# Relu-squared attention followed by a top-1 expert layer: TensorE's order given to the scheduler, score tiles made five ahead, some high parts on ScalarE, PSUM banks regrouped and the routing steps spread

## The chip, the cores and the metric

The kernel runs on one core of one Trainium2 chip. A core has a matrix engine (TensorE, PE in the profile), a vector engine (VectorE, DVE), a scalar engine (ScalarE, ACT), a general engine (GpSimd, POOL) and SyncE (SP), which in this kernel issues nearly all transfers. Matmuls write to PSUM, which has eight banks of 128 x 512 f32. The metric is the device time of one execution in microseconds. Where profiles are quoted, they come from one profiled execution, whose span runs from its first to its last instruction.

## The reference

B = 8 sequences of S = 2496 positions, 256 values wide, with 64-wide score vectors. Attention without a softmax feeds a layer of E = 8 experts with hidden width 1024, of which each position uses one:

```python
scores = (1.0 / S) * np.matmul(z, z.transpose(0, 2, 1))
attn = np.maximum(scores, 0.0) ** 2
x = (u * np.matmul(attn, v)).reshape(B * S, D)

xn = x / (np.linalg.norm(x, axis=-1, keepdims=True) + 1e-06)
logits = xn @ en.T / tau                 # en: normalised expert_emb
expert_idx = np.argmax(logits, axis=1)   # gate_w: its softmax probability
for e in range(E):
    mask = expert_idx == e
    h = np.maximum(x[mask] @ w1[e], 0.0)
    out[mask] = gate_w[mask, None] * (h @ w2[e])
```

## The kernel before

**Precision.** Matmuls run on f16 operands. Each f32 factor is kept as a sum of a high and a low f16 part, and a product is formed from three matmuls (high x high, high x low, low x high).

**Attention.** A sequence has NG = 5 groups of columns (four of 512, one of 448) and NST = 20 tiles of 128 rows. The main loop goes through `steps`, the 800 triples (b, g, s). In a step, `values` (L328) adds the product of value tile s with the probabilities of (s, g) to two accumulators, k = 0 and 1, of 512 columns: six matmuls (L339 to L341, or L336 and L337 for the last tile). The score matrix of a sequence is symmetric, so only tiles with s // 4 >= g are computed ("own" or direct steps: 20, 16, 12, 8 and 4 of a sequence's groups, 480 in all). The others are taken from `turned` tiles `tt`, which DMA transposes (L317) filled in an earlier group.

An own tile is made in two functions. `scores` (L294) issues two matmuls into a bank `sc` (L299, L300) and has ScalarE take the Relu into `a` (L302) and square it in place (L303). `parts` (L306) has VectorE cast the square to the high part (L309), subtract to get the low part (L310), and, where it is needed later, issues the transpose. At the start of a step the loop calls `scores` for the tile LOOK = 3 own tiles ahead; at its end it calls `parts` for the one LOOK - 1 ahead.

**PSUM.** Pool `psS` has four banks for `sc` and, in the expert stage, `po`; `psA` has three for the accumulators and, in the expert stage, `ph`; `psM` has one, `pm`, for small matmuls.

**Routing.** When a group is done, `route` (L351) returns some two dozen pieces with due times counted in steps: `gate_x` (times u, which reads both accumulators, L369), `squares` (L373), `total` (a `pm` matmul, L378), `scale`, `high` (L393), `low` (L396), `turn` (four transposes into `row`, L401), `logits` (`pm`, L407), `take`, `top`, `rank` (`pm`, L491), `place`, `sums`, four `norm` pieces, the square root, `exps`, `gates` and at 40 steps `scatters` (L516), indirect stores by GpSimd of the rows to an array `xs`, sorted by expert. The pieces wait in `queue`; the loop takes those that are due. Group g's pieces thus run beside the attention of the next groups.

**Beside it.** `ahead` spreads over a sequence the scans of the next sequence's z and v for their largest value, the scales from them (`pm` matmuls L130 and L146), and the loads and splits of z (`z_load` L189, `z_split` L202). Splits of v (`v_split`, L280 and L283) run in the last groups. The weights of the experts are read, split and stored back (`weights`, L526) in small pieces through the first seven sequences. `u_load` (L345) fetches the u of the next group.

**Experts.** Eleven steps before the end of attention `slot_first` (L950) loads the rows and weights of the first slots; a slot holds 256 or 128 rows of one expert. `slot_up` (L899) and `slot_down` (L924) then run slot by slot. Each calls `pop`, which runs one piece that is left in `queue`.

**Order.** The program is traced in the order of these loops. L1000 asks the scheduler to leave TensorE, ScalarE, VectorE and SyncE in just that order; GpSimd isn't in the list. An engine that isn't in it gets its order before the run from the scheduler, which takes of the instructions it holds to be ready the one that stands first in the program. Each engine's order is fixed when the kernel runs.

Of the kernel before, what the change touches and what calls it, by code (L numbers as in the profile page):

```python
# [7 lines left out]
F32 = mybir.dt.float32  # L8
F32R = mybir.dt.float32r
F16 = mybir.dt.float16  # L10
BF16 = mybir.dt.bfloat16
I32 = mybir.dt.int32
U32 = mybir.dt.uint32
AF = mybir.ActivationFunctionType
# [5 lines left out]
P = 128  # L20
TA, TB = 256, 128
ROW = 260
VAHEAD = 6
LOOK = 3
ZMAX, VMAX = 10, 7
SHIFT = 21
NSKIP = 4
# [18 lines left out]
def relu2_attention_then_moe(ctx, tc, zT, uT, v, emb, tau, w1, w2, ident, tri, iota_e, out):  # L46
# [13 lines left out]
    WR1, WR2 = 2 * W1, 2 * W2 + 8  # L60
    KA, KB = slot_counts(B, S, E)
    KT = KA + KB
    assert XFIRST <= NWB - 1 and NWB + 1 <= XAHEAD <= KA
    S2 = float(S) * float(S)
    twin = S % P == DQ
# [4 lines left out]
    dram = ctx.enter_context(tc.tile_pool(name="dram", bufs=1, space=DRAM))  # L70
    cst = ctx.enter_context(tc.tile_pool(name="cst", bufs=1))
    sml = ctx.enter_context(tc.tile_pool(name="sml", bufs=2))
    psS = ctx.enter_context(tc.tile_pool(name="psS", bufs=4, space=PSUM))
    psA = ctx.enter_context(tc.tile_pool(name="psA", bufs=3, space=PSUM))
    psM = ctx.enter_context(tc.tile_pool(name="psM", bufs=1, space=PSUM))

    xs = dram.tile([E * CAP + TB, ROW], F32, name="xs")
# [7 lines left out]
    zpool = actx.enter_context(tc.tile_pool(name="zpool", bufs=2))  # L85
    vring = actx.enter_context(tc.tile_pool(name="vring", bufs=NST + 5))
    wk = actx.enter_context(tc.tile_pool(name="wk", bufs=3))
    tp = actx.enter_context(tc.tile_pool(name="tp", bufs=min(7, max(1, NG * (NG - 1) // 2))))

    Zs = {}  # L90
    Vs = {}
# [202 lines left out]
    def scores(b, g, s):  # L294
        t0, n = groups[g]
        z1, z2 = Zs[b]
        sc = psS.tile([P, 512], F32, name="sc", tag="s")
        ss = slice(s * P, (s + 1) * P)
        nc.tensor.matmul(sc[:, :n], z1[:, ss], z1[:, t0:t0 + n], start=True, stop=False)  # L299
        nc.tensor.matmul(sc[:, :n], z1[:, ss], z2[:, t0:t0 + n], start=False, stop=True)  # L300
        a = wk.tile([P, 512], F32, name="a", tag="a")
        state["at"] = nc.scalar.activation(a[:, :n], sc[:, :n], AF.Relu, scale=2.0 ** -SHIFT).ins  # L302
        nc.scalar.activation(a[:, :n], a[:, :n], AF.Square)  # L303
        return a

    def parts(b, g, s, a):  # L306
        n = groups[g][1]
        hl = wk.tile([P, 2, 512], F16, name="hl_", tag="hl", bufs=5)
        state["dv"] = nc.vector.tensor_copy(hl[:, 0, :n], a[:, :n]).ins  # L309
        nc.vector.tensor_tensor(hl[:, 1, :n], a[:, :n], hl[:, 0, :n], op=ALU.subtract)  # L310
        h = s // GT
        if h > g:
            if (b, g, h) not in turned:
                turned[b, g, h] = tp.tile([P, 2 * GT, 512], F16, name="tt", tag="tt")
            m = min(P, S - s * P)
            c = (s % GT) * P
            nc.sync.dma_start_transpose(turned[b, g, h][:, :, c:c + m], hl[:m].rearrange("p a t -> p (a t)"))  # L317
        return hl[:, 0, :], hl[:, 1, :]
# [32 lines left out]
    def route(b, g, acc, ut):  # L351
# [7 lines left out]
            nc.gpsimd.memset(xhl[:, :, n:nj * P], 0.0)  # L359
        lg = rt.tile([P, 4, E], F32, name="lg", tag="lg")  # L360
        n2 = rt.tile([P, 4], F32, name="n2", tag="n2")
        row = rt.tile([P, 4, ROW + 4], F32, name="row", tag="row")
        rowi = row.bitcast(I32)
        row16 = row.bitcast(F16)
        loc = {}
# [81 lines left out]
            loc["ob"] = ob  # L447

        def sums():
            x = rt.tile([P, 4, D], F32, name="x", tag="x", bufs=1)  # L450
            nc.vector.tensor_tensor(x[:, :nj, :], row16[:, :nj, 0:D], row16[:, :nj, D:2 * D], op=ALU.add)
            loc["x"] = x

        def norm(j):
            def f():
                sq = rt.tile([P, D], BF16, name="sq", tag="sq", bufs=1)
                nc.scalar.activation(sq, loc["x"][:, j, :], AF.Square, accum_out=n2[:, j:j + 1])
            return f
# [37 lines left out]
        def place():  # L496
            ob, pm = loc["ob"], loc.pop("pm")
            state["pm"] = False
            old = state["carry"]
            pos = rt.tile([P, 4, E], F32, name="pos", tag="pos")  # L500
            nc.vector.tensor_tensor(pos[:, :nj, :], pm[:, 0:nj * E].rearrange("p (j e) -> p j e", e=E),
                                    old.unsqueeze(1).broadcast_to([P, nj, E]), op=ALU.add)
            new = sml.tile([P, E], F32, name="carry", bufs=3)
            nc.vector.tensor_tensor(new, pm[:, 4 * E:5 * E], old, op=ALU.add)
            state["carry"] = new
            nc.vector.tensor_tensor(pos[:, :nj, :], pos[:, :nj, :], ob[:, 4:4 + nj, :], op=ALU.mult)  # L506
            dst = rt.tile([P, 4], F32, name="dst", tag="dst")
            nc.vector.tensor_reduce(dst[:, :nj], pos[:, :nj, :], axis=AX.X, op=ALU.add)
            dsti = rt.tile([P, 4], U32, name="dsti", tag="dsti")
            nc.vector.tensor_copy(dsti[:, :nj], dst[:, :nj])  # L510
            loc["dsti"] = dsti

        def scatters():
            for j in range(nj):
# [2 lines left out]
                    xs[:, :], bass.IndirectOffsetOnAxis(ap=loc["dsti"][:m, j:j + 1], axis=0),  # L517
                    row[:m, j, 0:ROW], None)

        return [(0, gate_x), (2, squares), (5, total, True), (6, scale), (8, high), (9, low), (11, turn), (12, logits, True),  # L520
                (13, take), (14, top), (15, rest_scale), (17, rank, True), (18, place), (26, sums)] \
            + [(28 + j, norm(j)) for j in range(nj)] \
            + [(33, root), (34, roots), (35, shifted), (37, exps), (39, gates), (40, scatters)]


    def weights(e):  # L526
# [111 lines left out]
        first_max(c0)  # L638
    probs = {}
    halves = {}  # L640
    for i in range(min(LOOK, len(direct))):
        probs[direct[i]] = scores(*direct[i])
    for i in range(min(LOOK - 1, len(direct))):
        halves[direct[i]] = parts(*direct[i], probs.pop(direct[i]))
    zk = 2
    for k in range(3, min(5, ZN)):
        z_load(0, k * ZC)
    if ZN > 2:
        z_split(0, 2 * ZC)()
        zk = 3  # L650
    for f in scale_pieces(0, "v"):
        at_once(f)


    enhl = cst.tile([P, 2, 2 * E], F16, name="enhl")
    trib = cst.tile([P, P], BF16, name="trib")
    tri_f = sml.tile([P, P], F32, name="tri_f", bufs=1)
    nc.sync.dma_start(tri_f, tri)
    nc.vector.tensor_copy(trib, tri_f)
    ones_b = cst.tile([P, P], BF16, name="ones_b")  # L660
# [200 lines left out]
    mst = {}  # L861
    queue = []

    def pop():
        if queue:
            queue.pop(0)[1]()

    def slot_of(k):
        return (tables["A"], k, TA) if k < KA else (tables["B"], k - KA, TB)
# [108 lines left out]
    def ahead(b):  # L978

        todo = []  # L980
        at = min(4, NB // 16)
        for i, what in enumerate(SCANS):
            todo.append((at + 4 * i, False, lambda w=what: scan_load(b + 1, *w)))
            todo.append((at + 4 * i + 8, False, lambda w=what: scan_max(b + 1, *w)))
        at += 4 * len(SCANS) + 8
        for what, when in (("z", (0, 2, 6)), ("v", (6, 8, 14))):
            for j, (f, w) in enumerate(zip(scale_pieces(b + 1, what), when)):
                todo.append((at + w, j > 0, f))
        at += 10
        gap = max(1, (NB - early - at) // ZN)  # L990
        todo.append((0, False, lambda: z_tiles(b + 1)))
        for k in range(ZN):
            todo.append((max(0, at + (k - 3) * gap), False, lambda k=k: z_load(b + 1, k * ZC)))
            todo.append((at + k * gap, False, lambda k=k: z_split(b + 1, k * ZC)))
        return sorted(todo, key=lambda x: x[0])

    todo = []
    nd = 0
    ET = mybir.EngineType
    ctx.enter_context(tc.manual_schedule(engines={ET.PE, ET.Activation, ET.DVE, ET.SP}))  # L1000
    follow = []
    ready = min(3, NST)
    for s in range(ready):
# [6 lines left out]
    for i, (b, g, s) in enumerate(steps):  # L1010
# [12 lines left out]
            probs[st] = scores(*st)  # L1023
        if s == 0:
            accs[b, g] = [psA.tile([P, 512], F32, name=f"acc{k}", tag="a") for k in range(2)]
            nx = (b, g + 1) if g + 1 < NG else (b + 1, 0)
            if nx[0] < B:
                uts[nx] = u_load(*nx)
            if g == 0 and b + 1 < B:
                todo = ahead(b)  # L1030
        if b == 0 and g == 0 and s + ready < NST:
            follow.append(v_split(b, s + ready))
        if b + 1 < B:
# [16 lines left out]
        else:  # L1050
# [1 line left out]
            if s == 1 and NST > 2:  # L1052
                values(accs[b, g], b, g, 0, *late, ks=(1,))
            values(accs[b, g], b, g, s, *hv, ks=(1,))
        while queue and queue[0][0] <= i:
            pop()
        if wq and i >= wnext and (not wq[0][1] or pm_free(i)):
            wnext += wgap
            follow.append(wq.pop(0)[0]())
# [7 lines left out]
        if s == NST - 1:  # L1067
            queue += [(i + p[0], p[1], len(p) > 2) for p in route(b, g, accs.pop((b, g)), uts.pop((b, g)))]
            if b == B - 2 and g == NG - 1:
                queue.append((i + TABLE, table_a, False))  # L1070
            queue.sort(key=lambda x: x[0])
            pop()
        if own:
            if nd + LOOK - 1 < len(direct):
                st = direct[nd + LOOK - 1]
                halves[st] = parts(*st, probs.pop(st))
            nd += 1
    queue += [(len(steps) + TABLE, table_b, False), (len(steps) + TABLE, pads, False)]
    actx.close()
    slot_pools()  # L1080
    slot_w(1, 1)
# [7 lines left out]
    def work(k0, k1, load=True):  # L1089

        for k in range(k0, k1):
            if k + XAHEAD == KA:
                while queue:
                    pop()
            if k + XAHEAD < k1:
                slot_x(k + XAHEAD)
            slot_up(k)
            if k + NWB < k1:
                slot_w(k + NWB, 0)
            if k > k0:  # L1100
                slot_down(k - 1)
                if k - 1 + NWB < k1:
                    slot_w(k - 1 + NWB, 1)
        slot_down(k1 - 1)
# [79 lines left out]
```

## Time and profile before

| What | us |
|---|---|
| median of 3 runs (2266.07 to 2273.1) | 2268.45 |
| profiled execution | 2270.72 |
| its span, first to last instruction | 2268.8 |
| first value matmul of attention, from the span's start | 22.6 |
| first expert matmul | 1403.06 |
| TensorE, busy as the profile counts it | 2126.3 |
| VectorE busy | 1491.1 |
| ScalarE busy | 1116.7 |

Busy times are those of the whole span. A matmul of 512 columns stands in the profile with about 0.38 us, though the next one starts 0.216 us later; so starts are to be compared, not busy times. In a view of windows each row gives the stretch, its length, then for each engine busy time and number of instructions, the granted TensorE clock, the share of time in which the DMA engines were busy, and what they moved in GB/s. In a list of waits a row gives who waited for whom: total, times, longest. In a timeline a row gives start, duration, engine, line and operation, and in brackets the idle time of the engine before it.

### The profile page before, as it was taken

The numbers are of one execution on the slowest core, as the hardware profiler recorded it, in microseconds if no ns is written. First come the engines' busy times: TensorE is split into PE (matmuls) and PEld (weight loads), VectorE is DVE, ScalarE is ACT, GpSimd is POOL, SyncE is SP. The second block draws the span as 40 slices with busy tenths as digits, with TensorE's granted clock in tenths as the row PEclk, the third lists the DMA queues.
The fourth block names the chain that finished last, engine by engine and source line by source line (L and its number), as shares of the span: only waits on it lengthen the run. The fifth ranks groups of instructions, "written<-read, shape, count | busy, mean of one in ns | idle before, by whom it ended". The sixth has DMA issues, their size and how long they took to land. (4 is left out here: it accounts for less than half of the span.)

```text
span 2268.8 us, 43197 instructions
## 1 busy us (share of the span) xinstructions
PE 2126.3 (94%) x15154; PEld 1349.4 (59%) x15154; DVE 1491.1 (66%) x3972; ACT 1116.7 (49%) x2153; POOL 344.2 (15%) x428
## 2 busy tenths in 40 slices
PE   6998998999988989999999998999999999999997
PEld 2444444444444434444444444888888888889996
DVE  8887888979869879889888775543333333333332
ACT  7676576667747757767767753322222222222221
POOL 0011111011011111111111111132111111112111
PEclk9999999999999999999999999999999999999998
DMA  7967867876874974967885755642233332236561
GB/s 171 195 152 175 174 145 181 170 195 145 186 180 109 208 184 126 228 154 192 175 175 138 133 112 157 163 119 68 48 91 89 88 91 48 56 91 180 123 157 33
DMA packets 610316, 317.85 MB, mean 140 GB/s; under 512 B 530981, under 2 KB 573486, under 8 KB 602928
## 3 DMA queue, kind: packets, MB, share of 16 engines
q1 hardware_dynamic: 594912, 273.82, 53.7%
q0 software_dynamic: 15184, 41.24, 5.5%
q8 instruction: 121, 1.98, 0.4%
q14 instruction: 99, 0.81, 0.1%
HBM read 297.95 MB, written 59.60 MB: 158 GB/s over the span
## 5 line engine op out<-in xcount | busy, mean ns | idle before, releaser
L302 ACT ACTIVATE a<-sc 128x512 f32<-128x512 f32 (+1 forms) x480 | 282.8, 589 | 304.8 <-PE sc L300 175.1
L303 ACT ACTIVATE a<-a 128x512 f32<-128x512 f32 (+1 forms) x480 | 300.8, 627 | 15.1
L340 PEld LDWEIGHTS <-vv 128*128 128x128 f16 x1520 | 149.6, 98 | 233.2 <-issue 80.3
L341 PEld LDWEIGHTS <-vv 128*128 128x128 f16 x1520 | 149.7, 99 | 212.6 <-issue 54.4
L339 PE MATMUL acc<-tt,vv 128*128 128x512 f16 (+1 forms) x640 | 239.7, 375 | 28.9 <-DVE xt L369 22.6
L940 PE MATMUL po<-w,hl 128*128 128x256 f16 x944 | 257.3, 273 | 0.0
L938 PE MATMUL po<-w,hh 128*128 128x256 f16 x944 | 257.3, 273 | 0.0
L939 PE MATMUL po<-w,hh 128*128 128x256 f16 x944 | 257.3, 273 | 0.0
L339 PEld LDWEIGHTS <-vv 128*128 128x128 f16 x1520 | 149.7, 98 | 173.9 <-issue 6.8
L516 POOL DMA_INDIRECT xs<-row,dsti x160 | 172.4, 1078 | 502.1 <-DMA xs<-row,dsti 303.4
L945 POOL DMA_INDIRECT out_dram<-ot,mer x153 | 148.7, 972 | 615.9 <-DVE ot L944 378.2
L341 PE MATMUL acc<-tt,vv 128*128 128x512 f16 (+1 forms) x640 | 239.9, 375 | 0.0
L340 PE MATMUL acc<-tt,vv 128*128 128x512 f16 (+1 forms) x640 | 239.9, 375 | 0.0
L944 DVE TENSOR_SCALAR ot<-po,mer,w 128x256 f32<-128x256 f32 x114 | 58.1, 541 | 197.4 <-PE po L940 197.4
L299 PE MATMUL sc<-z 128*128 128x512 f16 (+1 forms) x480 | 183.1, 381 | 4.3 <-DVE z L215 4.3
L300 PE MATMUL sc<-z,z 128*128 128x512 f16 (+1 forms) x480 | 183.2, 382 | 0.0
L940 PEld LDWEIGHTS <-hl 128*128 128x128 f16 x1272 | 124.5, 98 | 14.4
L938 PEld LDWEIGHTS <-hh 128*128 128x128 f16 x1272 | 124.5, 98 | 14.0
L939 PEld LDWEIGHTS <-hh 128*128 128x128 f16 x1272 | 124.5, 98 | 13.9
L444 POOL MEMSET ob<- 128x72 bf16 x40 | 6.2, 158 | 661.0 <-DVE pos L506 578.5
L939 PE MATMUL po<-wb,hh 128*128 128x256 f16 x328 | 89.4, 273 | 0.0
L940 PE MATMUL po<-wb,hl 128*128 128x256 f16 x328 | 89.4, 273 | 0.0
(4162 smaller groups left out, 5116.9 us busy)
## 6 DMA issues: line engine op xcount, KB each, us to landing
w<-wsd SPq DMA_DIRECT2D x73, 1026.0 KB
wa<-wsd SPq DMA_DIRECT2D x50, 1024.0 KB
w<-wsd SPq DMA_DIRECT2D x48, 1024.0 KB
wb<-wsd SPq DMA_DIRECT2D x25, 1026.0 KB
scan<-in_v_dram SPq DMA_DIRECT2D x56, 312.0 KB
vt<-in_v_dram SPq DMA_DIRECT2D x133, 128.0 KB
ut<-in_uT_dram SPq DMA_DIRECT2D x32, 512.0 KB
wr<-in_w_dram SPq DMA_DIRECT2D x16, 1024.0 KB
```

The lines of the kernel that those rows point to most:

```text
L299: nc.tensor.matmul(sc[:, :n], z1[:, ss], z1[:, t0:t0 + n], start=True, stop=False)
L300: nc.tensor.matmul(sc[:, :n], z1[:, ss], z2[:, t0:t0 + n], start=False, stop=True)
L302: state["at"] = nc.scalar.activation(a[:, :n], sc[:, :n], AF.Relu, scale=2.0 ** -SHIFT).ins
L303: nc.scalar.activation(a[:, :n], a[:, :n], AF.Square)
L339: nc.tensor.matmul(acc[k][:, :n], va, ph[:, :n], start=first, stop=False)
L340: nc.tensor.matmul(acc[k][:, :n], va, pl[:, :n], start=False, stop=False)
L341: nc.tensor.matmul(acc[k][:, :n], vb, ph[:, :n], start=False, stop=last)
L516: nc.gpsimd.indirect_dma_start(xs[:, :], bass.IndirectOffsetOnAxis(ap=loc["dsti"][:m, j:j + 1], axis=0), row[:m, j, 0:ROW], None)
L938: nc.tensor.matmul(o, hh[:, f, t], wh, start=(f == 0), stop=False)
L939: nc.tensor.matmul(o, hh[:, f, t], wl, start=False, stop=False)
L940: nc.tensor.matmul(o, hl[:, f, t], wh, start=False, stop=(f == NF - 1))
L945: nc.gpsimd.indirect_dma_start(out, bass.IndirectOffsetOnAxis(ap=me.bitcast(U32)[:, j, 1:2], axis=0), ot[:, j, :], None, bounds_check=N - ...
```

## The change

- L1000: TensorE leaves the list of engines in program order; ScalarE, VectorE and SyncE stay.
- `LOOK` goes from 3 to 5: scores five own tiles ahead, parts four. The start of the kernel makes five and four tiles accordingly. Buffers: `a` from 3 to 5, `hl_` from 5 to 7, `tt` from 7 to 6.
- `hl_` is now allocated in `scores`; for tiles with s % 3 = 1 ScalarE writes the high part, with a second Square from `a` to f16, and VectorE's cast falls away.
- `psS` has three banks instead of four, `psA` four instead of three.
- The routing pieces lie further apart (`scatters` at 49 instead of 40), `rest_scale` comes before `take`; `row` and `dsti` get a third buffer.
- `u_load` is called at step 3 of a group instead of 0; `z_load` two steps later.
- In the expert stage a call of `pop` counts one step and runs what is due by then, where it ran one piece whatever its due time.
- Two small tiles are renamed or share a buffer.

```diff
-LOOK = 3
+LOOK = 5
...
-    psS = ctx.enter_context(tc.tile_pool(name="psS", bufs=4, space=PSUM))
-    psA = ctx.enter_context(tc.tile_pool(name="psA", bufs=3, space=PSUM))
+    psS = ctx.enter_context(tc.tile_pool(name="psS", bufs=3, space=PSUM))
+    psA = ctx.enter_context(tc.tile_pool(name="psA", bufs=4, space=PSUM))
...
-    tp = actx.enter_context(tc.tile_pool(name="tp", bufs=min(7, max(1, NG * (NG - 1) // 2))))
+    tp = actx.enter_context(tc.tile_pool(name="tp", bufs=min(6, max(1, NG * (NG - 1) // 2))))
...
-        a = wk.tile([P, 512], F32, name="a", tag="a")
-        state["at"] = nc.scalar.activation(a[:, :n], sc[:, :n], AF.Relu, scale=2.0 ** -SHIFT).ins
+        a = wk.tile([P, 512], F32, name="a", tag="a", bufs=LOOK)
+        nc.scalar.activation(a[:, :n], sc[:, :n], AF.Relu, scale=2.0 ** -SHIFT)
+        hl = wk.tile([P, 2, 512], F16, name="hl_", tag="hl", bufs=LOOK + 2)
+        if s % 3 == 1:
+            nc.scalar.activation(hl[:, 0, :n], a[:, :n], AF.Square)
         nc.scalar.activation(a[:, :n], a[:, :n], AF.Square)
-        return a
+        return a, hl
...
-        hl = wk.tile([P, 2, 512], F16, name="hl_", tag="hl", bufs=5)
-        state["dv"] = nc.vector.tensor_copy(hl[:, 0, :n], a[:, :n]).ins
+        a, hl = made
+        if s % 3 != 1:
+            nc.vector.tensor_copy(hl[:, 0, :n], a[:, :n])
         nc.vector.tensor_tensor(hl[:, 1, :n], a[:, :n], hl[:, 0, :n], op=ALU.subtract)
...
-        row = rt.tile([P, 4, ROW + 4], F32, name="row", tag="row")
+        row = rt.tile([P, 4, ROW + 4], F32, name="row", tag="row", bufs=3)
...
-            dsti = rt.tile([P, 4], U32, name="dsti", tag="dsti")
+            dsti = rt.tile([P, 4], U32, name="dsti", tag="dsti", bufs=3)
...
-        return [(0, gate_x), (2, squares), (5, total, True), (6, scale), (8, high), (9, low), (11, turn), (12, logits, True),
-                (13, take), (14, top), (15, rest_scale), (17, rank, True), (18, place), (26, sums)] \
-            + [(28 + j, norm(j)) for j in range(nj)] \
-            + [(33, root), (34, roots), (35, shifted), (37, exps), (39, gates), (40, scatters)]
+        return [(0, gate_x), (4, squares), (7, total, True), (9, scale), (11, high), (13, low), (15, turn), (17, logits, True),
+                (18, rest_scale), (19, take), (20, top), (23, rank, True), (25, place), (34, sums)] \
+            + [(36 + j, norm(j)) for j in range(nj)] \
+            + [(41, root), (42, roots), (43, shifted), (46, exps), (48, gates), (49, scatters)]
...
-    for i in range(min(LOOK, len(direct))):
+    for i in range(4):
         probs[direct[i]] = scores(*direct[i])
-    for i in range(min(LOOK - 1, len(direct))):
+    for i in range(3):
         halves[direct[i]] = parts(*direct[i], probs.pop(direct[i]))
...
+    probs[direct[4]] = scores(*direct[4])
+    halves[direct[3]] = parts(*direct[3], probs.pop(direct[3]))
     for f in scale_pieces(0, "v"):
         at_once(f)
...
+    def run(i):
+        while queue and queue[0][0] <= i:
+            queue.pop(0)[1]()
+
     def pop():
-        if queue:
-            queue.pop(0)[1]()
+        state["step"] += 1
+        run(state["step"])
...
-            todo.append((max(0, at + (k - 3) * gap), False, lambda k=k: z_load(b + 1, k * ZC)))
+            todo.append((max(0, at + (k - 3) * gap + 2), False, lambda k=k: z_load(b + 1, k * ZC)))
...
-    ctx.enter_context(tc.manual_schedule(engines={ET.PE, ET.Activation, ET.DVE, ET.SP}))
+    ctx.enter_context(tc.manual_schedule(engines={ET.Activation, ET.DVE, ET.SP}))
...
+        if s == min(3, NST - 1):
             nx = (b, g + 1) if g + 1 < NG else (b + 1, 0)
             if nx[0] < B:
                 uts[nx] = u_load(*nx)
...
+    state["step"] = len(steps) - 1
...
             if k + XAHEAD == KA:
-                while queue:
-                    pop()
+                run(1 << 30)
```

More of the change, by code (lines that the diff above doesn't have):

```diff
@@ L62, in relu2_attention_then_moe @@
     KT = KA + KB
+    assert LOOK == 5 and NST > LOOK
     assert XFIRST <= NWB - 1 and NWB + 1 <= XAHEAD <= KA
@@ L300, in scores, with parts @@
         nc.tensor.matmul(sc[:, :n], z1[:, ss], z2[:, t0:t0 + n], start=False, stop=True)
-        a = wk.tile([P, 512], F32, name="a", tag="a")
-        state["at"] = nc.scalar.activation(a[:, :n], sc[:, :n], AF.Relu, scale=2.0 ** -SHIFT).ins
+        a = wk.tile([P, 512], F32, name="a", tag="a", bufs=LOOK)
[3 more added lines that the diff above has]
+            nc.scalar.activation(hl[:, 0, :n], a[:, :n], AF.Square)
         nc.scalar.activation(a[:, :n], a[:, :n], AF.Square)
-        return a
-    def parts(b, g, s, a):
+        return a, hl
+    def parts(b, g, s, made):
         n = groups[g][1]
-        hl = wk.tile([P, 2, 512], F16, name="hl_", tag="hl", bufs=5)
-        state["dv"] = nc.vector.tensor_copy(hl[:, 0, :n], a[:, :n]).ins
+        a, hl = made
+        if s % 3 != 1:
+            nc.vector.tensor_copy(hl[:, 0, :n], a[:, :n])
         nc.vector.tensor_tensor(hl[:, 1, :n], a[:, :n], hl[:, 0, :n], op=ALU.subtract)
@@ L449, in sums @@
         def sums():
-            x = rt.tile([P, 4, D], F32, name="x", tag="x", bufs=1)
+            x = rt.tile([P, 4, D], F32, name="x", tag="xt", bufs=1)
             nc.vector.tensor_tensor(x[:, :nj, :], row16[:, :nj, 0:D], row16[:, :nj, D:2 * D], op=ALU.add)
@@ L640, in relu2_attention_then_moe @@
     halves = {}
-    for i in range(min(LOOK, len(direct))):
+    for i in range(4):
         probs[direct[i]] = scores(*direct[i])
-    for i in range(min(LOOK - 1, len(direct))):
+    for i in range(3):
         halves[direct[i]] = parts(*direct[i], probs.pop(direct[i]))
-    zk = 2
     for k in range(3, min(5, ZN)):
         z_load(0, k * ZC)
-    if ZN > 2:
-        z_split(0, 2 * ZC)()
-        zk = 3
+    z_split(0, 2 * ZC)()
+    zk = 3
+    probs[direct[4]] = scores(*direct[4])
+    halves[direct[3]] = parts(*direct[3], probs.pop(direct[3]))
     for f in scale_pieces(0, "v"):
@@ L656, in relu2_attention_then_moe @@
     trib = cst.tile([P, P], BF16, name="trib")
-    tri_f = sml.tile([P, P], F32, name="tri_f", bufs=1)
+    tri_f = sml.tile([P, P], F32, name="tri_f", tag="en", bufs=1)
     nc.sync.dma_start(tri_f, tri)
@@ L1025, in relu2_attention_then_moe @@
             accs[b, g] = [psA.tile([P, 512], F32, name=f"acc{k}", tag="a") for k in range(2)]
+            if g == 0 and b + 1 < B:
+                todo = ahead(b)
+        if s == min(3, NST - 1):
             nx = (b, g + 1) if g + 1 < NG else (b + 1, 0)
@@ L1028, in relu2_attention_then_moe @@
                 uts[nx] = u_load(*nx)
-            if g == 0 and b + 1 < B:
-                todo = ahead(b)
         if b == 0 and g == 0 and s + ready < NST:
@@ L1054, in relu2_attention_then_moe @@
             values(accs[b, g], b, g, s, *hv, ks=(1,))
-        while queue and queue[0][0] <= i:
-            pop()
+        run(i)
         if wq and i >= wnext and (not wq[0][1] or pm_free(i)):
@@ L1071, in relu2_attention_then_moe @@
             queue.sort(key=lambda x: x[0])
-            pop()
+            run(i)
         if own:
@@ L1092, in work @@
             if k + XAHEAD == KA:
-                while queue:
-                    pop()
+                run(1 << 30)
             if k + XAHEAD < k1:
```

## The prediction

> **What bounds the kernel now.** I began with the page's engine lines and its forty slices, to see which stage has room.
>
> ```profile
> span 2268.8 us, 43197 instructions
> PE 2126.3 (94%) x15154; PEld 1349.4 (59%) x15154; DVE 1491.1 (66%) x3972; ACT 1116.7 (49%) x2153; POOL 344.2 (15%) x428
> DVE  8887888979869879889888775543333333333332
> ```
>
> Two stages show: attention with its routing (VectorE at 8 to 9 tenths), and the expert stage (VectorE at 3). The 94% of TensorE says little, because a matmul's end is modelled and overlaps the next one's start. What counts is the distance between starts. So I took windows next: attention, the five groups of batch 5, and a stretch of the expert stage.
>
> ```profile
> core 0: us, PE busy (x) PEld busy (x) DVE busy (x) ACT busy (x) POOL busy (x), PEclk, DMA share, GB/s
> 22.60:1403.00 1380.40, 1280.98 (x6598) 586.27 (x6599) 1157.11 (x3355) 912.49 (x1798) 175.64 (x244) 0.99 0.72 165
> 904.70:943.50 38.80, 35.60 (x178) 15.73 (x178) 32.80 (x86) 28.71 (x54) 4.92 (x6) 1.00 0.86 183
> 943.50:979.90 36.40, 34.22 (x174) 15.16 (x173) 31.91 (x86) 23.24 (x46) 5.01 (x6) 1.00 1.01 238
> 979.90:1014.20 34.30, 32.72 (x172) 15.10 (x171) 29.91 (x95) 19.02 (x37) 5.15 (x7) 1.00 0.62 136
> 1014.20:1043.90 29.70, 29.70 (x160) 13.88 (x158) 25.76 (x80) 22.42 (x47) 3.73 (x6) 1.00 0.57 157
> 1043.90:1073.90 30.00, 27.52 (x152) 13.58 (x151) 28.41 (x89) 24.02 (x53) 6.06 (x9) 0.94 0.83 215
> 1520.00:2200.00 680.00, 680.00 (x6883) 617.21 (x6882) 243.94 (x388) 154.03 (x258) 128.24 (x132) 1.00 0.37 93
> ```
>
> The pitch of a matmul comes from the timeline, where the queue runs without a stop: 29 steps of 512 columns between the first two rows, one of 448 between the others.
>
> ```profile
> 1014.21 0.38 PE L339 MATMUL acc<-tt,vv 128*128 128x512 f16 x1
> ...
> 1020.47 0.38 PE L341 MATMUL acc<-tt,vv 128*128 128x512 f16 x1
> 702.99 0.35 PE L339 MATMUL acc<-tt,vv 128*128 128x448 f16 x1
> 703.18 0.35 PE L340 MATMUL acc<-tt,vv 128*128 128x448 f16 x1
> ```
>
> That is 6.26/29 = 0.216 us and 0.19 us. The counts are in the groups by line:
>
> ```profile
> L341 PEld LDWEIGHTS <-vv 128*128 128x128 f16 x1520 | 149.7, 99 | 212.6 <-issue 54.4
> L337 PEld LDWEIGHTS <-vv 128*128 128x128 f16 x80 | 7.8, 98 | 10.1 <-issue 1.6
> L299 PE MATMUL sc<-z 128*128 128x512 f16 (+1 forms) x480 | 183.1, 381 | 4.3 <-DVE z L215 4.3
> ```
>
> L339 and L340 run as often as L341, L336 as L337, L300 as L299: 4720 value and 960 score matmuls. One value group in five has 448 columns, and so have 64 score matmuls. So 4672 x 0.216 + 1008 x 0.19 = 1201 us. The other 6598 - 5680 = 918 matmuls are small; in group 3 of batch 5 (29.7 us, no stop) 134 large ones take 28.9, so 26 small ones take 0.8, or 0.03 each: 27 us. **TensorE needs 1228 us of the 1380; it stands still for 152.** In the expert stage it stands for none: 680 of 680 us at a pitch of 0.099. What the change can win lies in those 152 us, and at the handover.
>
> Who holds it up? By the same pitches, batch 5 stands about 4 us in group 0, 3 in group 1, 3 in group 2, none in group 3, 5 in group 4. A step of group 0 in batch 2 shows the commonest way:
>
> ```profile
> 402.24 0.38 PE L300 MATMUL sc<-z,z 128*128 128x512 f16 x1
> 402.88 0.42 DVE L309 CAST hl__4824<-a 128x512 f16<-128x512 f32 x1
> 403.36 0.38 PE L339 MATMUL acc<-hl__4824,vv 128*128 128x512 f16 x1 [0.74 <-DVE hl__4824 L309]
> 404.09 0.38 PE L340 MATMUL acc<-hl__4824,vv 128*128 128x512 f16 x1 [0.35 <-DVE hl__4824 L310]
> ```
>
> The value matmuls wait for the high part (L309), then for the low part (L310): starts come 1.12 and 0.73 us apart instead of 0.216, so 1.4 us of a step stand. VectorE is late because small routing instructions come ahead of the cast in its queue, and parts are made only two tiles ahead. Over a batch it isn't full (1157 us of 1380): this is latency and bursts. The list of waits names the rest:
>
> ```profile
> PE acc L339 <- DVE xt L369: 22.6, 17, 5.0
> PE pm L491 <- DVE ob L445: 7.5, 4, 5.6
> PE pm L378 <- ACT xhl L373: 7.3, 1, 7.3
> PE pm L146 <- DVE pos L506: 6.4, 2, 6.1
> ACT a L302 <- PE sc L300: 175.1, 174, 10.2
> SPq L401 <- DMA xs<-row,dsti: 95.0, 28, 10.2
> SPq L348 <- DVE hl__8813 L309: 11.2, 1, 11.2
> ```
>
> L339 behind L369 is the second accumulator of a new group: three banks hold one and a half pairs, so it waits until `gate_x` has read the old pair.
>
> **The change, part by part.**
>
> *Banks.* Four accumulator banks let a new pair start while `gate_x` reads the old one. The 22.6 us over 17 waits go; I take 22. The fourth score bank is given up: tile i+5 then needs tile i+2 read by its Relu. ScalarE waits 175 us for scores, so it is normally early; up to 10 us may come back, counted under ScalarE.
>
> *Five ahead.* Parts are made four direct tiles before their use instead of two. In group 0 that is 4 x 8 x 0.216 = 6.9 us of cover instead of 3.5. Buffers `a` and `hl_` grow with it; `tt` falls from seven to six, which is what a batch holds at once. Of the 152 us, 22 are the banks', some 20 belong to `pm` matmuls, and some 20 are half-speed clock (below): about 90 are waits of own steps on parts or split values. Bounds: 0 (VectorE remains the pace) to 90. I take 50, nearer the upper end, since the wait shown is shorter than the cover added.
>
> *A third of the high parts.* Tiles with s % 3 = 1 are 7, 6, 4, 3 and 2 of a batch's groups: 22 x 8 = 176. The rows:
>
> ```profile
> 0.00:1403.00 1403.00, 202.06 (x480) 0.99 0.72 166
> L303 ACT ACTIVATE a<-a 128x512 f32<-128x512 f32 (+1 forms) x480 | 300.8, 627 | 15.1
> ```
>
> The first is the windows view of L309 alone: 0.421 us a cast. VectorE loses 176 x 0.421 = 74 us. The added Square to f16 doesn't stand in the trace; the nearest row is the same Square to f32, 0.627 us, so ScalarE gains about 110 us (912 to 1023 of 1380). In group 0 it goes from 28.7 to 28.7 + 7 x 0.627 = 33.1 us against 34.7 that TensorE needs there: hidden, barely. Bursts won't all hide: I charge 10 us, with bounds 0 and 35 (all 7 x 8 = 56 such tiles of group 0 uncovered). The 74 us of VectorE are what makes the 50 above possible; they aren't counted again.
>
> A rule speaks against this edit. The Trainium skill, "ScalarE: Activation LUTs", section "Rules for kernel authors", gives plain arithmetic to VectorE, not ScalarE. The two rows agree that VectorE is quicker for one tile (0.42 against 0.63), so by that rule alone the edit would be a loss of some 36 us; I hold that the engine with idle time should pay, and the windows name ScalarE as that engine.
>
> *TensorE's order.* Program order still decides what is ready first, but a `pm` matmul or a score whose input is late no longer has to come before ready value matmuls, and the next group's first values may fill a hole. It is a fixed order made before the run, so it helps where the holes fall where they were expected. Of some 20 us of `pm` waits in attention I take 8. Bounds: plus 20 to a loss, below.
>
> *Wider steps* of the routing, third `row` and `dsti` buffers, `u_load` at step 3 instead of 0: VectorE's and ScalarE's work is the same, more spread; the 95 us in which SyncE's queue waits at L401 and the 11 us at L348 (one such wait in most batches) shrink. Behind them on SyncE stand `tt` transposes, `vt`, `zt` and `scan` loads. One u transfer is issued three steps later, still 37 steps before its `gate_x`. TensorE doesn't wait for these now: 0. The loads of z come two steps later, with seven steps left: 0.
>
> *The clock.* One `pm` wait, and the stretch right behind it:
>
> ```profile
> 706.46 0.27 PE L548 MATMUL pm<-idt,mx 128*2 128x128 f32 x1 [2.74 <-DVE h L386]
> 706.80:710.20 3.40, 3.40 (x11) 1.41 (x10) 2.64 (x9) 1.37 (x4) 1.08 (x2) 0.50 0.79 233
> core 0: 2268.8 us, clock 0.986
> ```
>
> Eleven matmuls in 3.4 us where 18 fit: 1.4 us lost by one wait. The third row, of the view of cores, says that 1.4% of the span's clock was withheld, 32 us, part of it in the idle ends; near 20 us in attention. Such dips go with the long waits; I take 10.
> The Trainium skill, "TensorE: Matmul & The Clock Gate", section "What's actually happening", has the clock halve after an idle window of about 3.4 us; here a 2.74 us wait was enough. By that figure only the longest waits would carry the penalty and the sum would win some 5 us less; the trace decides.
>
> *Start.* Two more tiles of parts and scores run before the scale of v: two tiles at 0.42 + 0.69 us, one without its cast, about 2 us later. I charge 2.
>
> *Handover.*
>
> ```profile
> 1388.42 1.04 POOL L516 DMA_INDIRECT xs<-row,dsti  x1 [1.68 <-DMA xs<-row,dsti]
> 1390.98 1.27 SPq L881 DMA_TRANSPOSE xt<-xs  x1
> 1403.06 0.27 PE L914 MATMUL ph__17242<-xt,wa 128*128 128x256 f16 x1
> ```
>
> The first expert load follows the scatter of group 1 of batch 7, 12 us before TensorE needs it. With scatters at due time 49 instead of 40 that scatter comes nine steps of six 0.19 us matmuls later, so that load, the weights behind it on SyncE and the next `turn` come about 10 us later. The cover of 12 us shrinks to 2, while the landing takes several. Against it `squares` moves behind four expert tiles, so the 7.3 us wait at L378 shortens. Bounds -7 to +12; I charge 5.
>
> *The sum*: -22 - 50 - 8 - 10 + 10 + 2 + 5 = -73 us. The profiled execution took 2270.7 us (span 2268.8 and 1.9 around it), so 2198 us. The median of the runs is 2268.45, 2.3 lower: **2195 us**.
>
> **The rivals.**
>
> *TensorE becomes the bound.* All waits but the first and last go: 152 - 15 left = -137, so 2131 us, range 2115 to 2160. For it: group 3 already runs so. Against it: VectorE would hold 1083 of about 1245 us with bursts.
>
> *Transfers become the bound in groups 0 and 1.* The DMA share is 0.86 and 1.01 in those two windows of batch 5. If they can't be compressed, gains stay in the last three groups, whose share is lower: the 22 us mostly, `pm`, half the clock: about -30, so 2238, range 2225 to 2262. Against it: over attention the share is 0.72.
>
> *No change* (waits only change their names: 2262 to 2275). That the order isn't changed at all isn't a rival of its own; banks and look-ahead act without it.
>
> ```profile
> L302 ACT ACTIVATE a<-sc 128x512 f32<-128x512 f32 (+1 forms) x480 | 282.8, 589 | 304.8 <-PE sc L300 175.1
> ```
>
> *Slower: a wrong place in the fixed order.* The row is ScalarE's Relu of a score tile, 0.589 us. TensorE does nothing while its next matmul waits, as in the rows at 402.24 and 403.36. If score pairs come before the chip has freed the third bank, everything behind waits for ScalarE's Relu. Each of the 480 own steps then pays w; it outweighs the 73 us from w = 0.15 us on. With w = 0.3, half of that Relu: +144 - 73, so 2340. Against it: ScalarE waits for scores far more than the reverse.
> The Trainium skill, same page, section "Step-by-step: what each phase is for", says only weight loads are pulled ahead and matmuls keep their order, so such a wait couldn't heal itself; the two rows agree.
>
> **How the numbers follow.** My forecast (2160 to 2225): 0.50. TensorE the bound: 0.14. Transfers the bound: 0.17. No change: 0.06. Slower: 0.13. A measurement of this kernel can tell about 0.3%, 7 us. Faster is 0.50 + 0.14 + 0.17 = 0.81, same 0.06, slower 0.13. The range leaves out the slower rival and the outer part of the first: 2130 to 2258.
>
> **What would show it.** Attention shorter by about 80 us, group 3 unchanged near 29.7 us, the expert stage unchanged. L339 no longer behind L369. The cast L309 runs 304 times in place of 480, and ScalarE has 176 more Squares. Group 0 of batch 5 near 36.5 us with ScalarE near 33. Few clock dips. At the handover L881 only a few us before the first L914. I am wrong if score matmuls (L299) wait for ScalarE, if DMA share stays near 1 while TensorE still waits, or if attention keeps its 1380 us with VectorE at 1083.

## The result and the profile after

| | before | changed |
|---|---|---|
| median of the runs, us | 2268.74 (2266.07 to 2273.1) | 2217.47 (2213.94 to 2220.85) |
| ratio, 95% interval | | 0.9772 (0.975 to 0.9794) |
| profiled execution, us | 2270.72 | 2217.79 |
| first value matmul to the end of the last one, us | 1380.4 | 1323.7 |
| from there to the end of the span, us | 865.7 | 867.6 |

The change takes 51 us off, 2.3%; 73 were forecast. The page of the changed kernel, engines and slices of VectorE, then the view of cores:

```profile
span 2215.6 us, 43233 instructions
PE 2105.5 (95%) x15154; PEld 1345.1 (61%) x15154; DVE 1421.2 (64%) x3796; ACT 1197.7 (54%) x2329; POOL 349.9 (16%) x428
DVE  7778878889888878788988864443333333333332
core 0: 2215.6 us, clock 0.988
```

All of it lies in attention: 56.7 us there, while start and expert stage cost 1.6 and 1.9 us more. The windows of the changed kernel at the same places (attention, the five groups of batch 5, the expert stage):

```profile
24.20:1348.00 1323.80, 1256.93 (x6589) 580.82 (x6589) 1081.91 (x3146) 990.48 (x1967) 182.08 (x244) 0.99 0.72 170
868.40:907.10 38.70, 36.30 (x182) 15.89 (x181) 31.14 (x82) 33.55 (x67) 6.89 (x11) 1.00 0.74 171
907.10:942.40 35.30, 33.04 (x173) 15.14 (x172) 28.84 (x78) 28.25 (x57) 4.47 (x6) 1.00 1.04 240
942.40:979.10 36.70, 34.09 (x171) 15.41 (x170) 30.48 (x98) 22.23 (x45) 4.50 (x6) 0.95 0.63 144
979.10:1008.90 29.80, 29.80 (x160) 13.94 (x159) 24.60 (x77) 21.48 (x43) 4.83 (x6) 1.00 0.74 165
1008.90:1038.10 29.20, 26.62 (x149) 13.20 (x148) 26.05 (x79) 22.40 (x50) 3.03 (x4) 0.94 0.67 173
1520.00:2160.00 640.00, 640.00 (x6569) 581.99 (x6567) 230.10 (x365) 144.73 (x243) 119.51 (x123) 1.00 0.37 96
```

VectorE holds 1082 us there in place of 1157, ScalarE 990 in place of 912. Group 3 and the expert stage (640/6569, 0.097 us a matmul) are as they were. Group 1 runs at a DMA share of 1.04 and is none the slower for it. By itself batch 5 gained little; over the eight batches the groups took 295, 283, 279, 241 and 226 us after 311, 294, 286, 242 and 247.

Where TensorE still stands is in the list of waits of the changed kernel. These are rows from it, the last one ScalarE's (`wsd` holds the split weights of the experts):

```profile
PE pm L383 <- DVE pos L511: 37.2, 15, 7.0
PE sc L300 <- ACT a L303: 6.6, 10, 1.5
PE ph__17184 L923 <- DMA wa<-wsd: 4.6, 1, 4.6
PE ph__19315 L923 <- DMA wa<-wsd: 3.8, 1, 3.8
PE pm L496 <- DVE ob L450: 3.4, 5, 1.2
ACT a L303 <- PE sc L301: 105.8, 89, 8.3
```

The wait for `gate_x` (before, L339 behind L369) is gone, and the largest row left of a value matmul is 2.6 us. At the top is one that had no such weight before: L383 is `total`, L511 stands in `place`.

The list hides short waits, since matmuls' ends are modelled. So I added up, for every kernel of this study, by how much each matmul started later than the pitch of the one before allows (0.42 ns a column, at least 62 ns; 20 ns or less not counted), sorted by the matmul that came late, from the first value matmul to 30 us behind the last. A half clock is in it. "Values from tt" means value matmuls that read a transposed tile: these wait for an accumulator bank, for split values, or run at half clock. Two more columns split the profiled execution: "attention" runs from the start of the first value matmul to the start of the last, "behind" from there to the end of the span. They come from one execution of each kernel, the medians from four or more.

| kernel | us, median | ratio to before (95%) | attention | behind | values from parts | values from tt | scores | `total` | `rank` | other pm | sum |
|---|---|---|---|---|---|---|---|---|---|---|
| before | 2268.74 | 1 | 1380.3 | 865.9 | 83 | 44 | 3 | 7 | 8 | 20 | 166 |
| changed | 2217.47 | 0.9772 (0.975 to 0.9794) | 1323.6 | 867.8 | 16 | 10 | 12 | 41 | 8 | 15 | 110 |
| pe_manual | 2248.78 | 0.9923 (0.99 to 0.9946) | 1352.0 | 869.5 | 3 | 24 | 17 | 53 | 7 | 30 | 142 |
| look3 | 2272.11 | 1.0027 (1.0013 to 1.0042) | 1391.6 | 863.1 | 65 | 21 | 14 | 32 | 7 | 33 | 179 |
| banks_back | 2219.45 | 0.9793 (0.9763 to 0.9823) | 1322.9 | 867.3 | 22 | 28 | 8 | 14 | 17 | 12 | 108 |
| all_dve | 2216.44 | 0.9784 (0.9758 to 0.9809) | 1325.3 | 867.4 | 21 | 11 | 7 | 43 | 6 | 17 | 112 |
| before_pe_free | 2246.61 | 0.9913 (0.9891 to 0.9935) | 1357.6 | 862.5 | 68 | 34 | 3 | 7 | 2 | 27 | 144 |
| before_look5 | 2246.01 | 0.9894 (0.9864 to 0.9925) | 1358.3 | 861.7 | 16 | 76 | 12 | 8 | 11 | 21 | 146 |
| bl5_free | 2228.92 | 0.9833 (0.9814 to 0.9853) | 1337.2 | 864.2 | 16 | 59 | 3 | 7 | 11 | 26 | 124 |
| bl5_banks | 2233.45 | 0.9838 (0.9821 to 0.9855) | 1344.5 | 865.2 | 14 | 12 | 17 | 13 | 15 | 58 | 130 |
| place22 | 2209.39 | 0.9737 (0.9713 to 0.9761) | 1314.2 | 871.2 | 15 | 8 | 5 | 13 | 4 | 48 | 100 |
| t10_11_12 | 2203.60 | 0.9713 (0.969 to 0.9736) | 1315.9 | 863.1 | 21 | 8 | 15 | 11 | 9 | 28 | 103 |
| t10_dve | 2212.92 | 0.9741 (0.9715 to 0.9767) | 1322.8 | 866.2 | 33 | 6 | 10 | 5 | 6 | 40 | 110 |
| t10_banks | 2213.68 | 0.976 (0.9744 to 0.9776) | 1315.3 | 871.1 | 20 | 27 | 7 | 2 | 17 | 19 | 100 |

The few us of expert matmuls are in the sum alone. Each ratio is against runs of the kernel before on the same chip; the medians of these were 2266.25 to 2269.28 us.

### The profile page after: what moved, and what is told of

Its sections match the earlier page's. It is cut to its first block, busy times and chain, and to the rows that moved or that the text cites. A ratio compares the mean times of both kernels' runs of the same rounds, so it can differ in the third digit from the quotient of the medians.

```text
span 2215.6 us, 43233 instructions
## 1 busy us (share of the span) xinstructions
PE 2105.5 (95%) x15154; PEld 1345.1 (61%) x15154; DVE 1421.2 (64%) x3796; ACT 1197.7 (54%) x2329; POOL 349.9 (16%) x428
## 5 line engine op out<-in xcount | busy, mean ns | idle before, releaser
L303 ACT ACTIVATE a<-sc 128x512 f32<-128x512 f32 (+1 forms) x480 | 278.1, 580 | 109.3 <-PE sc L301 105.8
```

## The experiments

### Four parts of the change undone, one at a time

**TensorE in program order again.**

```diff
-    ctx.enter_context(tc.manual_schedule(engines={ET.Activation, ET.DVE, ET.SP}))
+    ctx.enter_context(tc.manual_schedule(engines={ET.PE, ET.Activation, ET.DVE, ET.SP}))
```

> The changed kernel with TensorE put back into the list of engines that keep program order; nothing else differs. Theory A (look-ahead and banks bring the gain, the scheduler's order little, as the 8 us of the prediction): 2217 to 2232 us, about 2225, and the waits of value matmuls for parts stay as short as in the changed kernel (some 15 us of standing). Rival B (the scheduler's order is the main source of the 51 us): 2245 us or more, with long stands in front of pm matmuls and value matmuls.

2248.78 us, in the range of rival B: 31 us of the 51 are gone, four times what I had given the order. 28 us of the 31 lie in attention. The values hardly wait for parts any more (3 us), yet `total` stands 53 us and the other pm matmuls 30. So the wait at `total` doesn't come from the scheduler's order; program order has it too, and longer. In the views of waits and cores of this kernel:

```profile
PE pm L383 <- DVE pos L511: 51.0, 15, 7.3
PE pm L131 <- DVE spwz L153: 17.1, 7, 3.1
core 0: 2245.6 us, clock 0.980
```

The clock may have a part in it. (1 - 0.980) x 2245.6 = 45 us of clock are withheld against (1 - 0.988) x 2215.6 = 27 in the changed kernel. The 18 us between are at most what the clock costs of the 31, as half a clock costs nothing while TensorE stands. In the profiled executions the three kernels with look-ahead five and program order have 0.980, 0.981 and 0.981, the eight with look-ahead five and the freed order 0.985 to 0.989; over all executions the two ranges meet (0.976 to 0.987 and 0.983 to 0.992). At look-ahead three there is no such order: 0.986 before, 0.987 in `before_pe_free`, 0.978 in `look3`. That a freed order spares the clock is thus not shown.

**Look-ahead three again.**

```diff
-LOOK = 5
+LOOK = 3
...
-    for i in range(4):
+    for i in range(3):
         probs[direct[i]] = scores(*direct[i])
-    for i in range(3):
+    for i in range(2):
         halves[direct[i]] = parts(*direct[i], probs.pop(direct[i]))
...
-    probs[direct[4]] = scores(*direct[4])
-    halves[direct[3]] = parts(*direct[3], probs.pop(direct[3]))
```

> The changed kernel with scores three and parts two own tiles ahead again, and the start as before; buffers a and hl_ follow (3 and 5), the rest stays. Theory A: the waits of own steps on the high and low parts come back, about 50 us, so 2260 to 2270. Rival B (scheduler's order or the lighter VectorE would do without more look-ahead): at most 2230.

2272.11 us, 2 us above theory A's range and 0.3% above the kernel before. The waits of values for parts come back (65 us), as theory A has it, and rival B falls. That it is 25 us slower than `before_pe_free` below, which also has look-ahead three and a free TensorE, means that the other edits (banks, casts, wider steps, later loads) together cost time at this look-ahead. Which of them does so I didn't separate; `hl_` is also taken one stage earlier here, with five buffers as before. So the 55 us between it and the changed kernel aren't the worth of the look-ahead alone.

**Banks as before.**

```diff
-    psS = ctx.enter_context(tc.tile_pool(name="psS", bufs=3, space=PSUM))
-    psA = ctx.enter_context(tc.tile_pool(name="psA", bufs=4, space=PSUM))
+    psS = ctx.enter_context(tc.tile_pool(name="psS", bufs=4, space=PSUM))
+    psA = ctx.enter_context(tc.tile_pool(name="psA", bufs=3, space=PSUM))
```

> The changed kernel with four score banks and three accumulator banks again. Theory A: the second accumulator of each new group waits for gate_x again (some 30 us of standing before), the score waits for a bank (about 10 us) go: 2235 to 2245. Rival (TensorE's free order hides the missing bank, the score banks matter as much): 2210 to 2225.

2219.45 us: no difference that can be told, inside the rival's range. Theory A's range begins 16 us above, and the list of waits says why:

```profile
PE acc L344 <- DVE xt L374: 18.9, 14, 5.6
PE pm L496 <- DVE ob L450: 13.3, 10, 3.6
PE pm L383 <- DVE pos L511: 11.9, 9, 2.6
```

The wait for `gate_x` is back, and `total` waits 12 us where it waited 37. In the table, values from tt, `total` and `rank` come to 28 + 14 + 17 = 59 us, and in the changed kernel to 10 + 41 + 8 = 59. Attention is as long as before the edit (1322.9 and 1323.6 us). At a group's start TensorE waits for VectorE; here the bank only settles which matmul does the waiting.

**All casts on VectorE.**

```diff
-        if s % 3 == 1:
-            nc.scalar.activation(hl[:, 0, :n], a[:, :n], AF.Square)
...
-        if s % 3 != 1:
-            nc.vector.tensor_copy(hl[:, 0, :n], a[:, :n])
+        nc.vector.tensor_copy(hl[:, 0, :n], a[:, :n])
```

> The changed kernel with every high part cast by VectorE again: 480 casts, 176 fewer Squares on ScalarE. Theory A as the prediction had it (the 74 us taken from VectorE are what makes the look-ahead pay): 2235 to 2250, with value matmuls waiting for parts. Rival C (VectorE has room once the latency is covered, and ScalarE's 110 us cost about as much as they bring): 2208 to 2226.

2216.44 us, rival C. In the changed kernel the windows of the cast and of the Square to f16 show that the work did move as forecast, 0.625 us for each new Square:

```profile
0.00:1348.00 1348.00, 127.86 (x304) 0.99 0.72 170
0.00:1348.00 1348.00, 110.00 (x176) 0.99 0.72 170
```

So 74 us less on VectorE, 110 more on ScalarE, and no time for it: with parts four tiles ahead the cast isn't what TensorE waits for.

### Parts of the change alone

**TensorE free, nothing else** (the line of `pe_manual` the other way, in the kernel before).

> The kernel before with one word changed: TensorE left to the scheduler, look-ahead three, banks 4 and 3, all else as before. In the changed kernel the freed order is worth 31 us. Theory E (parts add up): 2235. Theory D (a freed order pays only where enough tiles are ready to fill a hole, so it needs the look-ahead): 2255 to 2272.

2246.61 us, 22 us faster. Neither number fits: the time lies between the two. The freed order pays without more look-ahead, so theory D falls, but less than the 31 us that it is worth inside the change, which theory E took. Parts still wait (68 us after 83).

**Look-ahead five, nothing else** (LOOK, the buffers of `a`, `hl_` and `tt`, and the start as in the changed kernel).

> The kernel before with the look-ahead of five alone (buffers a, hl_ and tt and the start as in the changed kernel; TensorE in program order, banks 4 and 3, old steps, all casts on VectorE). In the changed kernel the look-ahead is worth 55 us. Theory E (parts add up): 2212. Theory D (look-ahead and order need each other): 2235 to 2255, with the second accumulator's wait for gate_x (L339 behind L369) unchanged near 20 us and the waits for parts mostly gone.

2246.01 us, 23 us. The waits for parts fall from 83 to 16, more than the gain. Half goes back at the accumulators; in its list of waits the row that stood at 22.6 us is now

```profile
PE acc L339 <- DVE xt L369: 58.9, 27, 4.5
```

Theory D had the time right and this row wrong. A reading that I didn't test: parts that are made earlier are work that VectorE does ahead of `gate_x`.

**Both together, and look-ahead with the banks** (`bl5_free`: the two edits above; `bl5_banks`: look-ahead five, `psS` 3, `psA` 4, program order).

> The kernel before with two edits of the change: look-ahead five and TensorE left to the scheduler. Old steps, banks 4 and 3, all casts on VectorE. Alone they were worth 23 and 22 us. Theory I (these two carry the whole gain, the other edits add nothing in sum): 2212 to 2226. Rival J (wider steps, banks or the third of the casts are needed beside them): 2235 or more. If below 2205, the other edits cost time.

> The kernel before with look-ahead five and the banks exchanged (four for accumulators, three for scores), TensorE in program order, old steps, all casts on VectorE. With look-ahead five and three accumulator banks, L339 stood 59 us behind gate_x (L369). Theory K (under program order that bank is what takes the look-ahead's gain away): that wait goes and the time falls by 30 to 45 us to 2200 to 2215. Rival H (VectorE is late at a group's start whatever waits for it): L369's wait goes, but the next matmul that needs VectorE (total, rank or a score) takes it over, 2230 to 2246.

2228.92 and 2233.45 us. The two main edits give 40 us, nearly the sum of their 22 and 23; with the order freed, the look-ahead is worth 18. The rest of the change adds 11 us to that (0.9772 against 0.9833, intervals apart), so theory I is short and rival J too high. For the banks under program order rival H holds: values from tt fall from 76 to 12 us, but scores and pm matmuls take 103 where they took 52, and about 13 us are won in place of 30 to 45.

### The new wait

`total` needs the one pm bank. With the wider steps the previous group's `place`, which reads it, is due at 25, step 5 of the new group, two steps ahead of `total` at 7; before, it was due at 18, ahead of the group's end. One such wait of the changed kernel, in group 4 of batch 2 (timeline, rows of TensorE and VectorE):

```profile
514.32 0.35 PE L345 MATMUL acc<-tt,vv 128*128 128x448 f16 x1
516.89 0.19 DVE L506 TENSOR_TENSOR pos<-pm,carry 128x32 f32<-128x32 f32 x1
517.00 0.15 DVE L509 TENSOR_TENSOR carry<-pm,carry 128x8 f32<-128x8 f32 x1
517.30 0.16 PE L383 MATMUL pm<-ssq,ones_b 128*128 128x1 bf16 x1 [2.62 <-DVE pos L511]
```

L509 is the last reader of the bank, and `total` starts 0.15 us after it ends. The values behind `total` then start 0.19 us apart, with no wait of their own. VectorE comes late to `place`: up to 516.85 us it works at splits of v and z that stand ahead of it in its own order. Two kernels move the two apart, one from each side:

```diff
-        return [(0, gate_x), (4, squares), (7, total, True), (9, scale), (11, high), (13, low), (15, turn), (17, logits, True),
-                (18, rest_scale), (19, take), (20, top), (23, rank, True), (25, place), (34, sums)] \
+        return [(0, gate_x), (4, squares), (7, total, True), (9, scale), (11, high), (13, low), (14, turn), (15, logits, True),
+                (16, rest_scale), (17, take), (18, top), (20, rank, True), (22, place), (34, sums)] \
```

> The changed kernel with turn to place moved up by one to three steps (turn 14, logits 15, rest_scale 16, take 17, top 18, rank 20, place 22 in place of 15, 17, 18, 19, 20, 23, 25). The previous group's place then comes at step 2 of a group, five before total instead of two. Theory F (total, L383, waits for the pm bank that place, L511, still reads): its 41 us of standing fall by half or more, and the time to 2185 to 2205. Rival G (total waits for squares on ScalarE, held back by the transfer out of xhl): L383 unchanged, 2212 to 2225. Rival H (VectorE is late at a group's start whatever waits for it): L383 falls, but another wait takes its place, 2208 to 2222.

```diff
-        return [(0, gate_x), (4, squares), (7, total, True), (9, scale), (11, high), (13, low), (15, turn), (17, logits, True),
+        return [(0, gate_x), (4, squares), (10, total, True), (11, scale), (12, high), (13, low), (15, turn), (17, logits, True),
```

> The changed kernel with total at 10, scale at 11, high at 12 in place of 7, 9, 11. Total then comes five steps behind the previous group's place and six behind squares. Theory F: L383's wait falls by half or more, 2190 to 2208, a little of it given back by VectorE's scale, now one step behind total. Rival H (VectorE late at a group's start): another wait takes its place, 2208 to 2222.

```profile
PE pm L412 <- DVE xhl L401: 17.1, 10, 3.2
PE pm L383 <- DVE pos L511: 7.7, 6, 1.7
```

These two rows are of `place22`, 2209.39 us; the next is of `t10_11_12`, 2203.60 us.

```profile
PE pm L383 <- DVE pos L511: 8.6, 7, 2.0
```

Both cut the wait at `total` from 37 to about 8 us though `squares` stands where it stood, so rival G falls and theory F holds for this wait. For the time it holds in part. `place22` lies in rival H's range, and in both kernels other pm matmuls take over much of the wait (48 and 29 us after 15; in `place22` it is `logits`, L412, now two steps behind `low`). The sum falls from 110 to 100 and 103, and attention gets shorter by 9 us in `place22` and by 8 in `t10_11_12`.

So the two are alike in attention; what parts them lies behind it. These rows are of `place22`, `t10_11_12` and `t10_banks` (below), in this order:

```profile
PE ph__18222 L923 <- DMA w<-wsd: 6.2, 1, 6.2
PE ph__17184 L923 <- DMA wa<-wsd: 3.5, 1, 3.5
PE ph__19315 L923 <- DMA wa<-wsd: 4.2, 1, 4.2
```

They are expert matmuls that wait for their weights. All of TensorE's waits from 1330 us on come to 11.0 us in the changed kernel, 15.0 in `place22` and 6.8 in `t10_11_12`, most of each for weights. The column "behind" has 867.8, 871.2 and 863.1, the same differences within 0.6 us. Of the 14 us that `t10_11_12` wins, some 8 are thus won in attention and some 5 behind it, where TensorE waits less for weights; no run shows why they come sooner. Its interval (0.969 to 0.9736) lies below that of the changed kernel, and its median is the lowest of the study.

**The same with casts and banks undone** (`t10_11_12` with the edits of `all_dve` and of `banks_back`).

> The changed kernel with total at 10, scale at 11, high at 12, and all casts on VectorE. Theory C (once parts are made four tiles ahead, it doesn't matter which engine casts): 2196 to 2211, the same as with the third on ScalarE. Rival: with the pm wait shorter VectorE is what counts again, 2215 or more.

> The changed kernel with total at 10, scale at 11, high at 12, and four score banks, three accumulator banks. With total at 7 the banks made no difference, as the wait for gate_x stood in place of the wait at total. Theory H (one wait for a late VectorE a group, whatever its name): 2203 plus the wait that total no longer takes, 2212 to 2222. Rival (the freed order does without the fourth accumulator bank): 2197 to 2210.

2212.92 and 2213.68 us. For the casts the time lies between the two forecasts and the intervals overlap, so 9 us are likely and not settled; attention is 7 us longer, and values wait 33 us for parts in place of 21. For the banks the intervals part at the edge (0.9736 and 0.9744), and the time is in theory H's range, but its reason isn't what the profile shows: attention is as long as in `t10_11_12` (1315.3 and 1315.9 us). There the wait for `gate_x` is back (values from tt 27 us after 8, `rank` 17 after 9), and `total` and the other pm matmuls wait less by as much (2 + 19 us after 11 + 29). The 8 us lie behind attention (871.1 after 863.1), where TensorE waits 13.7 us after 6.8: 10.6 for weights of the experts, where it was 6.8, and 3.1 for VectorE to read a bank of `ph` (L923 behind L928), a wait that `t10_11_12` doesn't have. Pool `psA` holds `ph` too, with one bank less here. So in attention, with `total` moved, the bank again only settles which matmul waits; what it saves is seen in the expert stage, some 3 us.

## Why the prediction came out as it did

The direction and the range were right, and the stage too: 1228 us that TensorE needs, 152 in which it stood, and all of the gain from those. That the sum came within 22 us is in part luck, since terms that were wrong by 10 to 23 us have opposite signs (the banks on one side, casts and TensorE's order on the other). By terms:

- *Five ahead*, -50: the waits for parts fell by 67 us, from 83 to 16. Alone the edit brings 23 us, as the saved waits partly move to `gate_x`, 18 beside a freed order. Taken out of the change it costs 55, for which the other edits count too. Group 0 of batch 5 took 38.7 us and not 36.5, but 36.8 on average over the eight batches.
- *Banks*, -22: the row L339 behind L369 vanished, as read, and gave nothing that can be told, since `total` waits for the same engine at the same place; in program order with look-ahead five the banks bring 13 us. I took the price of a wait from its row without asking what VectorE was late with.
- *A third of the high parts*, +10 and "what makes the 50 possible": the durations were right (0.421 and 0.625 us), neither consequence shown; no effect within the intervals.
- *TensorE's order*, -8: 22 us alone, 31 within the change. Its size was wrong, by a factor of three to four, and the place named for it (late pm matmuls that no longer hold up ready ones) is right in part. Inside the change the stands at all pm matmuls fall from 90 us to 64; alone they don't fall (36 after 35), and the values gain instead (102 after 127).
- *Wider steps*, 0: **this is the step that failed.** I set out what the new due times do to SyncE and the handover, and not that `place` of one group lands two steps ahead of `total` of the next on a single pm bank. At `total` TensorE stands 41 us where it stood 7, and moving `total` wins back 8 us in attention. How much of the 22 us between forecast and result this explains stays open: no run undoes the wider steps alone, the stand at `total` is in part one that moved there (values from tt stand 59 us in `bl5_free`, 10 in the changed kernel), and the -22 that I took for the banks are as large.
- *The clock*, -10: 0.986 became 0.988, 32 us withheld became 27.
- *Start*, +2: 1.6 measured. *Handover*, +5: the first expert matmul waits 4.6 us for its weights, as forecast, and the 7.3 us at L378 shrank; in sum the rest of the kernel is 1.9 us longer.
- *z loads two steps later*, 0: ScalarE now waits for them, 20.9 us over 12 waits. TensorE doesn't show it.

```profile
L211 ACT ACTIVATE z<-zt,scz 64x256 f16<-64x256 f32 x80 | 39.7, 497 | 33.3 <-DMA zt<-in_zT_dram 20.9 <-DVE scz L155 10.2 <-DVE xh L691 2.0
```

Of the rivals, transfers as the bound: no; at a share of 1.04 group 1 fell from 36.4 to 35.3 us. The wrong place in the fixed order, the slower rival, isn't seen: scores stand 12 us, of which 6.6 for ScalarE's Relu, and the 41 us at `total` are 53 in program order.

## What to carry over

A wait in the profile is priced by its cause: where several matmuls in a row need the same late engine, taking away the resource of one hands the wait to the next, and only the sum over that place counts. When steps are spread, look for every pair that shares a single buffer across the iterations that now overlap. Parts of a change can be judged only beside the others: the look-ahead was worth 23 us alone, 18 beside a freed order and 55 taken out of the whole, the banks 13 us in program order and nothing that can be told in the changed kernel. And a difference in time is to be looked up in its stage: the 8 us that the PSUM banks seemed to bring with `total` moved lay in waits of the expert stage.

## What the runs showed of the hardware

A transpose right behind large loads can take SyncE several times longer to issue. The 320 `tt` transposes of the changed kernel take 1.26 us in the median. The four longest, 6.9, 5.1, 4.5 and 4.2 us, each came within three issues behind a pair of 1 MB weight loads (`wr`); after another such pair it was 1.2 us. In the longest case the four transposes of `turn` followed with 6.3 us; `squares` then waited 9.6 us for `xhl`, a scan load came late, VectorE stood 9.2 us at its reduction, and `place` and `total` behind it:

```profile
761.58 1.23 SPq L322 DMA_TRANSPOSE tt<-hl__9477  x1
762.86 0.57 SPq L536 DMA_DIRECT2D wr<-in_w_dram  x1
763.48 0.46 SPq L537 DMA_DIRECT2D wr<-in_w_dram  x1
764.05 6.89 SPq L322 DMA_TRANSPOSE tt<-hl__9494  x1
771.12 6.32 SPq L406 DMA_TRANSPOSE row<-xhl  x4
778.74 1.06 ACT L378 ACTIVATE xhl<-xt 128x1024 f16<-128x1024 f32 x1 [9.60 <-DMA row<-xhl]
783.48 0.80 DVE L114 TENSOR_REDUCE smxv<-scan 128x1 f32<-128x624 f32 x1 [9.18 <-DMA scan<-in_v_dram]
784.60 0.16 PE L383 MATMUL pm<-ssq,ones_b 128*128 128x1 bf16 x1 [7.00 <-DVE pos L511]
```

That is the longest stand in the list of waits of the changed kernel. It wasn't tried whether smaller weight loads avoid it.
